# Preparing the first feed-forward tile one row group per block instead of in seven neighbouring segments

## The chip, the cores and the metric

The kernel runs on one core of a Trainium2 chip. The metric is the device time of one execution in microseconds. The core has five instruction streams that the profile shows: PE (matrix products), DVE (VectorE), ACT (ScalarE), POOL (GpSimd) and SP (SyncE, which here issues nearly all DMAs). Each stream runs its instructions in the order in which the program writes them; streams meet through semaphores.

## What is computed

A transformer layer on 2048 rows of width 640 in bf16. First comes an attention with a recurrent memory: the rows are cut into 64 segments of 32, each segment is put behind 8 memory rows, and the first 8 rows of its output are the memory of the next segment. So segment s+1 can't begin its projections of the memory rows before segment s has its output.

```python
for s in range(n_seg):                       # 64 segments of 32 rows, one after the other
    h = concat([mem, x_ln[s*32:(s+1)*32]])   # 8 + 32 rows
    q, k, v = h @ Wq, h @ Wk, h @ Wv         # 32 heads of 128
    o = softmax(mask(q @ k.T * scale)) @ v @ Wo
    mem = o[:8]; outs.append(o[8:])
h  = x + concat(outs)
h2 = h + (relu(layernorm(h) @ w1 + b1) ** 2) @ w2 + b2     # 640 -> 1728 -> 640
```

Both layer norms are over the 640 columns of a row, without gain or bias.

## The kernel before, in words

**Segments and blocks.** Four segments make a block of 128 rows (16 blocks, loop over `b` at L911, over `sp` 0 to 3 below it; the segment number is `i = 4*b + sp`). A call of `step(b, sp)` writes the instructions of one segment. Its main chain goes: projections q and k on PE, evacuated by ACT into `row` and turned by DVE into `qT` and `kT`; POOL spreads `qT` into `qz`; PE makes the scores of the memory rows (`sm`); DVE and ACT make the softmax; PE multiplies by the values (`po`) and by the output weights (`pw`); and DVE and ACT turn the new memory into the operand of the next segment (`otr`, `otc`, `hT`, L294 to L297). A segment's stretch of time is counted here from its predecessor's first `otr` to its own.

**Queues of small work.** Work that is not in that chain stands in Python lists of closures, run at fixed places of `step`: `fill` holds PE work (the rows of each segment whose keys and values do not depend on the memory are projected a block ahead in the first, second and third segments; the fourth has the output product of the block before), `late` is emptied near the start of a step (L469: two items at the start, ten in blocks 0, 14 and 15; L552: one more after the first two projections; L560: the rest before the last), and `mid` gives two items at the end of a step (L678), after the instructions that hand the memory to the next segment. So what stands in `mid` in segment i runs at the start of the stretch of segment i+1, between `rk` (L653) and `o` (L285). `soon` gives one closure before each step (L913). The layer norm of block b+1's input has its statistics in `late` of the first segment of block b, its normalisation (`ln_norm`, L188, into `xn`) in `late` of the second and its DMA transpose (L193) before the third. In the second segment `tails_v_in` (L417) issues four loads into `vt`, in the third `load_x` one.

**The first feed-forward tile.** The feed-forward part works on tiles of 512 rows (`NT`), each of four groups of 128 (`NK4`). The rows of the first tile have been known since block 3, and while the attention still runs they are prepared. One group k takes five steps, and the loop at L956 says in which segments they are put: `prep_load` (SP: two DMAs, the attention's rows from `o_all`, L764, and the input rows, L765); one segment later `prep_sum` at the step's end (DVE, 128x640, L771); two segments later the statistics near the start (`stats`: DVE two `BATCH_NORM_STATS2` L170 and one aggregate L172, then POOL two operations on 128x1, L174 and L175) and the normalisation at the end (DVE, L776, into `hn`); three segments later, before the step, the DMA transpose into `hnT0` (SP, L193). `hn` takes the same single buffer as `xn` (tag `xn` in a pool of one), so a normalisation of either kind waits until the transpose of the one before has read it. From the end of segment 60 on, `early_units` computes three columns of the first feed-forward product from `hnT0` as `fill`.

Of the kernel before, what the change touches and what calls it, by code (L numbers as in the profile page):

```python
# [16 lines left out]
def kernel(  # L17
# [28 lines left out]
    NS = S // SEG  # L46
# [89 lines left out]
    def load_x(b, eng=nc.sync):  # L136
        xt = s2.tile([128, D], BF16, tag="xt", name="xt")
        r0 = b * 128 - (M if b else 0)
        eng.dma_start(out=xt[:], in_=x2d[r0:r0 + 128, :])
        xts[b] = xt  # L140
# [40 lines left out]
    def ln_stats(b):  # L181
        xns[b] = stats(xts[b][:])

    def ln_norm(b):
        mv, rs = xns[b]
        xn = s1.tile([128, D], BF16, tag="xn", name="xn")
        xt = xts.pop(b)
        nc.vector.tensor_scalar(out=xn[:], in0=xt[:], scalar1=mv[:, 0:1], scalar2=rs[:, 0:1],  # L188
                                op0=ALU.subtract, op1=ALU.mult)
        xns[b] = xn  # L190
# [4 lines left out]
    def ln_turn(b):  # L195

        xn = xns.pop(b)
        if isinstance(b, tuple):
            hTt = ht0[2][:].rearrange("p (c b k s) -> p c b k s", c=DC, b=4, k=TL)
            dma_transpose(hTt.rearrange("p c b k s -> p c (b k s)"), xn[:])  # L200
            hTts[b[1]] = hTt
            return
        if b not in hT4s:
            hT4s[b] = s2.tile([128, DC, 4, SEG], BF16, tag="hT4", name="hT4")
        dma_transpose(hT4s[b][:].rearrange("p c s t -> p c (s t)"), xn[:])
# [95 lines left out]
    def run(q, n):  # L301
        while n > 0 and q:
            q.pop(0)()
            n -= 1
# [4 lines left out]
    def tail_units(b, which, tiles=(mmtile, mmtile)):  # L309
        w = {"q": wq, "k": wk, "v": wv}[which]  # L310
        lhs = lambda c: tail_rows(b, c)
        st = {}

        def unit(n, c):
            def f():
                if c == 0:
                    st[n] = tiles[n]()
                proj(w, "columns" if which != "v" else "order", lhs, n, st[n], c, c + 1)
                if c == DC - 1:
                    tail_out(b, which, n, st[n][:])  # L320
            return f
        return [unit(n, c) for n in range(2) for c in range(DC)]

    def tail_quarters(b, which, n, u):
        if which == "v":
            wr = wv[:].rearrange("p (c k n u f) -> p c n k u f", c=DC, k=G, n=2, u=2)
            cols = lambda c, k: wr[:, c, n, k, u]
        else:
            w = {"q": wq, "k": wk}[which]
            wr = w[:].rearrange("p (c g j n k e) -> p c n k g j e", c=DC, g=G, n=2, j=4, k=4)  # L330
            cols = lambda c, k: wr[:, c, n, k, 2 * u:2 * u + 2]
        st = {}

        def unit(cs):
            def f():
                if 0 in cs:
                    st["ps"] = mmtile()
                for c in cs:
                    for k in range(4):
                        matmul(st["ps"][32 * k:32 * k + 32, 0:256], lhsT=tail_rows(b, c), rhs=cols(c, k),  # L340
                               start=(c == 0), stop=(c == DC - 1))
                if DC - 1 in cs:
                    row = spare.pop(0) if spare else rowtile()
                    evac_row(which, row[:, 0:256], st["ps"][:, 0:256])
                    if which == "v":
                        nc.sync.dma_start(out=vt_d[b, 2 * n + u], in_=row[:, 0:256])
                        return
                    dst = tails[b][which]
                    late.append(lambda: nc.vector.transpose(out=dst[:, n * 16 + u * 8:n * 16 + u * 8 + 8, 0:32],
                                                            in_=row[:, 0:256].rearrange("p (h e) -> p h e", e=32)))  # L350
            return f
        return [unit(cs) for cs in ((0, 1), (2, 3), (4,))]
# [22 lines left out]
    def wo_tail_units(b, tile_=mmtile):  # L375
        st = {}

        def out():
            o = wo_out(st["ps"])
            dst = o_all[:].rearrange("(b s t) d -> b s t d", s=4, t=SEG)  # L380
            for ch in range(2):
                nc.sync.dma_start(out=dst[b, :, HD:SEG, ch * DH:(ch + 1) * DH], in_=o[32 * ch:32 * ch + 32, :])

        def unit(k):
            def f():
                if k == 0:
                    st["ps"] = tile_()
                wo_rounds(lambda p: oTts[b % 2][:, p, :], st["ps"], k * 16 // 10, (k + 1) * 16 // 10)
                if k == 9:
                    late.append(out)  # L390
            return f
        return [unit(k) for k in range(10)]
# [304 lines left out]
    def ffn_biases():  # L697
        nc.sync.dma_start(out=b1b[:, 0:FFULL], in_=B_b1[0:FFULL * 128].rearrange("(c p) -> p c", p=128))
        for hh in range(2):
            nc.sync.dma_start(out=b1b[FREM * hh:FREM * (hh + 1), FFULL:FC],  # L700
                              in_=B_b1[FFULL * 128:F].rearrange("(p o) -> p o", o=1))
# [111 lines left out]
    def prep_sum0(k):  # L813
        pre[k] = prep_sum(0, k, pre[k])

    def prep_stats0(k):
        pre[k] = (pre[k], stats(pre[k]))

    def prep_norm0(k):
        hn = prep_norm(0, k, pre[k][0], *pre[k][1])  # L820
        soon.append(lambda: prep_turn(0, k, hn))
# [89 lines left out]
    for b in range(NB):  # L911
        for sp in range(4):
            run(soon, 1)  # L913
            if sp == 2 and b + 2 < NB:
                load_x(b + 2)
            if b == 0:
                for h in range((3, 1, 1, 1)[sp]):
                    fill += halves.pop(0)
                if sp:
                    fill += tail_quarters(*quarters.pop(0))  # L920
                if sp < 3:
                    soon.append(lambda n=(8, 5, 5)[sp]: [stores.pop()() for _ in range(min(len(stores), n))])
                if sp == 1:
                    late.append(lambda: ln_stats(("t", 3)))
                    mid.append(lambda: ln_norm(("t", 3)))
                if sp == 2:
                    ln_turn(("t", 3))
                    late.append(lambda: ln_stats(1))
                    mid.append(lambda: ln_norm(1))
                if sp == 3:  # L930
                    ln_turn(1)
                    spare += [hnT0[:, c, :] for c in range(2)]
            elif b < NB - 1:
                if sp == 0:
                    fill += tail_units(b + 1, "q")[0:DC] + tail_quarters(b + 1, "q", 1, 0)
                if sp == 1:
                    parts = tail_units(b + 1, "k")
                    fill += tail_quarters(b + 1, "q", 1, 1) + parts[0:DC]
                if sp == 2:
                    fill += parts[DC:]  # L940
                    if quarters:
                        fill += tail_quarters(*quarters.pop(0))
            if sp == 3 and b > 0:
                fill += wo_tail_units(b - 1)
            if b > 0 and sp == 0 and b + 1 < NB:
                late.append(lambda b=b: ln_stats(b + 1))
            if b > 0 and sp == 1 and b + 1 < NB:
                late.append(lambda b=b: ln_norm(b + 1))
            if b > 0 and sp == 2 and b + 1 < NB:
                ln_turn(b + 1)  # L950
            i = b * 4 + sp
            if (b, sp) == (1, 0):
                ffn_biases()
            if (b, sp) == (2, 2):
                nc.gpsimd.tensor_copy(out=b1f[:], in_=b1b[:])
            for k in range(NK4):  # L956
                at = NS - 12 + k + k // 3
                if i == at:
                    pre[k] = prep_load(0, k)
                if i == at + 1:  # L960
                    mid.append(lambda k=k: prep_sum0(k))
                if i == at + 2:
                    late.append(lambda k=k: prep_stats0(k))
                    mid.append(lambda k=k: prep_norm0(k))
            if i == NS - 4:
                early_places()
            if NS - 4 <= i < NS - 1:
                fill += early_units(i - (NS - 4))
            step(b, sp, v0 if b + sp == 0 else None)
# [23 lines left out]
    for t in range(S // NT):  # L993
# [6 lines left out]
        for fc in range(0 if t else NE, FC):  # L1000
# [14 lines left out]
            if more and fc >= first and (fc - first) // 3 < NK4:  # L1015
                k, stage = divmod(fc - first, 3)
# [16 lines left out]
        for q in range(NK4):  # L1033
# [8 lines left out]
            for hh in range(2):  # L1042
                k = pr + 2 * hh
# [46 lines left out]
```

## Time and profile before

| | us |
|---|---|
| median of three executions | 954.45 (953.89, 954.45, 956.87) |
| the profiled execution | 954.3 |
| its span, first to last instruction | 952.5 |
| PE busy in the span | 928.0 |
| DVE, ACT, POOL busy | 700.6, 545.6, 258.1 |
| granted TensorE clock, mean | 0.996 |
| the four `hn` normalisations begin | 713.3 to 765.2 |

The page of the profile shows busy time for each engine, the chain of work that ended last (followed back from the last instruction to what released each step), and groups of instructions by line, with the idle time of the engine before them and what ended it. The trace behind it can be asked for busy time in any stretch of time, for the chain in order of time, and for the instructions in order of time. L-numbers are lines of the kernel. `q8` is the DMA queue that fetched instruction code most (202 packets, 3.31 MB).

### The profile page before, as it was taken

The numbers are of one execution on the slowest core, as the hardware profiler recorded it, in microseconds if no ns is written. First come the engines' busy times: TensorE is split into PE (matmuls) and PEld (weight loads), VectorE is DVE, ScalarE is ACT, GpSimd is POOL, SyncE is SP. The second block draws the span as 40 slices with busy tenths as digits, with TensorE's granted clock in tenths as the row PEclk, the third lists the DMA queues.
The fourth block names the chain that finished last, engine by engine and source line by source line (L and its number), as shares of the span: only waits on it lengthen the run. The fifth ranks groups of instructions, "written<-read, shape, count | busy, mean of one in ns | idle before, by whom it ended". The sixth has DMA issues, their size and how long they took to land.

```text
span 952.5 us, 57527 instructions
## 1 busy us (share of the span) xinstructions
PE 928.0 (97%) x25861; PEld 574.9 (60%) x25873; DVE 700.6 (74%) x2136; ACT 545.6 (57%) x1342; POOL 258.1 (27%) x798
## 2 busy tenths in 40 slices
PE   6989999999999999999999999999999999999998
PEld 2455766666666666666666566666665566555555
DVE  3267888888888888888888888888888777476532
ACT  2546666666666666666666666666665666523321
POOL 1013222222222222222222222222223322164300
PEclk9989999999999999999999999999999999999999
DMA  9973210101010101010101010101021110463220
GB/s 352 398 245 91 46 29 17 27 13 30 14 29 10 34 11 33 9 35 9 34 9 34 9 34 9 34 10 31 25 59 39 32 36 7 133 174 90 90 56 29
DMA packets 63334, 57.23 MB, mean 60 GB/s; under 512 B 29544, under 2 KB 59248, under 8 KB 61168
## 3 DMA queue, kind: packets, MB, share of 16 engines
q1 hardware_dynamic: 62400, 53.23, 18.6%
q8 instruction: 202, 3.31, 1.5%
q14 instruction: 44, 0.36, 0.1%
q10 hardware_dynamic: 688, 0.33, 0.1%
HBM read 38.86 MB, written 9.44 MB: 51 GB/s over the span
## 4 chain that ended last, share of the span: by engine, by line
PE 88%; DMA 5%; DVE 3%; ACT 1%; SPq 1%; issue 1%; DVEq 0%; ACTq 0%
PE ps L114 59%; PE pw L114 16%; PE y L114 6%; PE po L114 5%; DMA wv<-in_A_Wv_dram 1%; DMA vt_d<-row 1%; PE sm L114 1%; DMA wo<-in_A_Wo_dram 1%; DMA vt<-vt_d 1%; SPq L163 1%; DVE qT L266 1%; DVE kT L489 0%; ACT row L263 0%; DVE kT L266 0%; ACT row L261 0%
## 5 line engine op out<-in xcount | busy, mean ns | idle before, releaser
L114 PEld LDWEIGHTS <-hT 128*32 128x32 bf16 x8348 | 222.5, 96 | 128.2 <-DVE hT L297 6.1
L114 PE MATMUL pw<-wo,oT 128*32 128x320 bf16 x4224 | 181.0, 302 | 3.3 <-DMA wo<-in_A_Wo_dram 2.9
L114 PE MATMUL ps<-wv,hT 128*32 128x512 bf16 x2520 | 177.6, 380 | 0.0
L114 PE MATMUL ps<-wq,hT 128*32 128x512 bf16 (+1 forms) x3138 | 160.2, 337 | 0.3 <-DVE hT L297 0.3
L114 PE MATMUL ps<-wk,hT 128*32 128x512 bf16 (+1 forms) x2570 | 159.7, 375 | 0.1
L114 PEld LDWEIGHTS <-oT 128*32 128x32 bf16 x4224 | 97.6, 96 | 58.9 <-DVE oT L252 20.1
L655 POOL TENSOR_TENSOR pkt<-ek,rk 128x64 bf16<-128x64 bf16 x64 | 19.1, 299 | 413.2 <-DVE rk L653 413.2
L261 ACT ACTIVATE row<-ps 128x512 bf16<-128x512 f32 (+1 forms) x170 | 94.0, 562 | 12.4 <-PE ps L114 8.8
L266 DVE STREAM_TRANSPOSE qT<-row 128x512 bf16<-128x512 bf16 x128 | 89.8, 701 | 9.7 <-ACT row L261 6.2
L443 ACT CAST oT<-po 128x512 bf16<-128x512 f32 x128 | 74.8, 587 | 0.0
L1012 ACT ACTIVATE wv<-ps,b1f 128x512 bf16<-128x512 f32 (+1 forms) x53 | 35.4, 672 | 65.3 <-PE ps L114 62.8
L295 ACT COPY otc<-otr 64x40 f32<-64x40 f32 x126 | 28.0, 222 | 69.7 <-DVE otr L294 69.1
L454 POOL COPY qz<-qT 128x96 bf16<-128x96 bf16 x126 | 33.4, 265 | 118.6 <-DVE mx L505 59.6
L114 PEld LDWEIGHTS <-hTt 128*32 128x32 bf16 x1660 | 46.4, 98 | 31.3 <-issue 3.6
L114 PEld LDWEIGHTS <-v 32*128 32x128 bf16 x4064 | 42.3, 91 | 32.8 <-issue 18.6
L263 ACT CAST row<-ps 128x512 bf16<-128x512 f32 (+1 forms) x111 | 60.2, 558 | 1.6 <-PE ps L114 0.8
L629 DVE TENSOR_REDUCE zk<-ek 128x8 f32<-128x320 bf16 x64 | 31.1, 486 | 38.1 <-ACT ek L628 38.1
L114 PE MATMUL y<-wq,wk 128*128 128x320 bf16 (+1 forms) x424 | 59.0, 300 | 0.0
L486 ACT CAST row<-ps 128x256 bf16<-128x256 f32 x126 | 40.7, 375 | 30.8 <-PE ps L114 30.8
L611 ACT CAST v<-ps 128x512 bf16<-128x512 f32 x63 | 36.9, 585 | 29.7 <-PE ps L114 29.7
L114 PEld LDWEIGHTS <-qz 128*32 128x32 bf16 x2016 | 36.6, 95 | 28.4 <-POOL qz L454 4.7
L266 DVE STREAM_TRANSPOSE kT<-row 128x512 bf16<-128x512 bf16 x65 | 45.7, 702 | 10.2 <-ACT row L263 7.5
(125 smaller groups left out, 1634.0 us busy)
## 6 DMA issues: line engine op xcount, KB each, us to landing
wv<-in_A_Wv_dram SPq DMA_DIRECT2D x5, 1024.0 KB
wq<-in_A_Wq_dram SPq DMA_DIRECT2D x5, 1024.0 KB
wk<-in_A_Wk_dram SPq DMA_DIRECT2D x5, 1024.0 KB
vt<-vt_d SPq DMA_DIRECT2D x60, 64.0 KB
xt<-in_A_x_dram SPq DMA_DIRECT2D x18, 160.0 KB
wo<-in_A_Wo_dram SPq DMA_DIRECT2D x2, 1280.0 KB
wq<-in_B_w_dram SPq DMA_DIRECT2D x1, 2080.0 KB
o_all<-o SPq DMA_DIRECT2D x128, 15.0 KB
```

The lines of the kernel that those rows point to most:

```text
L114: nc.tensor.matmul(*a, **k)
L261: nc.scalar.mul(out=row, in_=ps, mul=scale)
L263: nc.scalar.copy(out=row, in_=ps)
L266: nc.vector.transpose(out=dst[:, n * 16:(n + 1) * 16, 0:32], in_=row.rearrange("p (h e) -> p h e", e=32))
L295: nc.scalar.copy(out=tc_[:, a], in_=tr[64:128, a, :, 0:M])
L443: nc.scalar.copy(out=oTg[:, n, :, :, M:NK], in_=po[:, :, n * 128:(n + 1) * 128].rearrange("p g (j q) -> p g j q", q=32))
L454: nc.gpsimd.tensor_copy(out=d.rearrange("p a (j f) -> p a j f", j=3)[:, :, :, 0:M], in_=src[:, :, 0:3, :])
L486: nc.scalar.copy(out=row[:, u * 256:(u + 1) * 256], in_=ps[:, u * 256:(u + 1) * 256])
L611: nc.scalar.copy(out=v[:, 512:1024], in_=ps1[:])
L629: nc.vector.tensor_reduce(out=zk[:], in_=ek[:], op=ALU.add, axis=AX.X)
L655: nc.gpsimd.tensor_tensor(out=pkt[:], in0=ek[:, :, SEG:NK], in1=rk[:].unsqueeze(2).to_broadcast([128, HG, TL]), op=ALU.mult)
L1012: nc.scalar.activation(out=r[:, 0:w], in_=ps[:, 0:w], func=ACT.Relu, bias=b1f[:, fc:fc + 1], scale=1.0)
```

## The change

The segment in which group k's steps begin is set by one line. Before, `at = NS - 12 + k + k // 3` with `NS = 64` gave 52, 53, 54 and 56. Now it gives 45, 49, 53 and 57, always the second segment of blocks 11, 12, 13 and 14:

```diff
             for k in range(NK4):
-                at = NS - 12 + k + k // 3
+                at = NS - 19 + 4 * k
                 if i == at:
                     pre[k] = prep_load(0, k)
                 if i == at + 1:
                     mid.append(lambda k=k: prep_sum0(k))
                 if i == at + 2:
                     late.append(lambda k=k: prep_stats0(k))
                     mid.append(lambda k=k: prep_norm0(k))
```

| step of group k = 0, 1, 2, 3 | segments before | segments after |
|---|---|---|
| two loads, before the step | 52, 53, 54, 56 | 45, 49, 53, 57 |
| sum, at the end | 53, 54, 55, 57 | 46, 50, 54, 58 |
| statistics, near the start; normalisation, at the end | 54, 55, 56, 58 | 47, 51, 55, 59 |
| transpose, before the step | 55, 56, 57, 59 | 48, 52, 56, 60 |

The functions that the steps call, with what they compute and into which buffers, stay as they are.

## The prediction

> **What bounds the kernel now.** The page first: PE is busy nearly throughout, and the chain that ended last is PE's for 88%.
>
> ```profile
> span 952.5 us, 57527 instructions
> PE 928.0 (97%) x25861; PEld 574.9 (60%) x25873; DVE 700.6 (74%) x2136; ACT 545.6 (57%) x1342; POOL 258.1 (27%) x798
> ...
> PE 88%; DMA 5%; DVE 3%; ACT 1%; SPq 1%; issue 1%; DVEq 0%; ACTq 0%
> ```
>
> So moving DVE work can pay only where PE stood still for it. The second view is busy time by stretch, one stretch for each segment from 46 to 59, cut at each first `otr`. The columns are the stretch, its length, then busy time and instructions of PE, PEld, DVE, ACT and POOL, the clock, the DMA share and GB/s.
>
> ```profile
> 603.53:615.56 12.03, 11.95 (x387) 7.08 (x379) 9.84 (x31) 7.78 (x20) 3.17 (x11) 1.00 0.19 35
> 615.56:627.62 12.06, 12.06 (x400) 9.49 (x396) 9.45 (x30) 7.79 (x20) 3.15 (x11) 1.00 0.05 13
> 627.62:639.92 12.30, 12.30 (x392) 7.12 (x387) 9.97 (x32) 7.36 (x19) 3.90 (x13) 1.00 0.04 10
> 639.92:651.73 11.81, 11.81 (x388) 7.20 (x383) 9.81 (x31) 7.81 (x20) 3.17 (x11) 1.00 0.09 29
> 651.73:663.54 11.81, 11.81 (x386) 7.06 (x378) 9.83 (x30) 7.77 (x20) 3.16 (x11) 1.00 0.16 35
> 663.54:675.48 11.94, 11.94 (x399) 7.70 (x395) 9.45 (x30) 7.78 (x20) 3.17 (x11) 1.00 0.05 12
> 675.48:687.64 12.16, 12.16 (x391) 7.23 (x386) 9.85 (x32) 7.36 (x19) 3.89 (x13) 1.00 0.13 37
> 687.64:699.65 12.01, 12.01 (x390) 9.23 (x385) 9.89 (x32) 7.81 (x20) 3.17 (x11) 1.00 0.19 56
> 699.65:712.09 12.44, 12.17 (x386) 7.03 (x378) 10.87 (x34) 7.67 (x20) 3.98 (x13) 1.00 0.23 60
> 712.09:724.14 12.05, 12.00 (x400) 7.86 (x396) 10.54 (x34) 7.77 (x20) 4.18 (x13) 1.00 0.12 26
> 724.14:737.69 13.55, 12.41 (x391) 7.51 (x386) 11.54 (x37) 7.17 (x19) 4.97 (x15) 1.00 0.18 45
> 737.69:751.97 14.28, 12.05 (x388) 7.42 (x383) 10.06 (x32) 7.81 (x20) 3.19 (x11) 1.00 0.14 36
> 751.97:763.99 12.02, 11.95 (x386) 7.25 (x378) 10.60 (x34) 7.78 (x20) 3.97 (x13) 1.00 0.12 21
> 763.99:775.88 11.89, 11.58 (x399) 7.61 (x395) 9.76 (x30) 7.50 (x19) 3.19 (x11) 1.00 0.10 21
> ```
>
> From 46 to 53 PE is never idle for more than 0.08 us a stretch. In 54 to 58 it stands 0.27 + 0.05 + 1.14 + 2.23 + 0.07 = 3.76 us. The last line, segment 59, is short although it carries a normalisation. Third, the chain in order of time in segment 57, the worst:
>
> ```profile
> 738.99 0.32 DVE hn L776
> ...
> 740.58 2.66 DMA hnT<-hn
> ...
> 743.68 0.06 DVE xn L188
> ```
>
> Group 2's transpose is issued at the start of segment 57, where the block's own `ln_norm` wants the same single buffer. DVE waits 2.7 us for it, with the `qT` and `kT` turns queued behind.
>
> **The change, part by part.**
>
> What it removes. The five stretches 54 to 58 last 12.44 + 12.05 + 13.55 + 14.28 + 12.02 = 64.34 us. Undisturbed stretches of the same kinds are, from the table, third segment 12.03 or 11.81, fourth 12.06 or 11.94, first 12.30 or 12.16, second 11.81 or 12.01. With the longer of each the five would take 60.43, with the shorter 59.53: they give back 3.9 to 4.8 us. I take the middle, 4.36, since which of the two belongs to which place follows the code's position and I can't tell it. Two causes lie in it: the transpose wait of 57 (14.28 against 11.91, 2.4 us), and in 54 to 56 too much DVE work at once. Segment 56 takes a normalisation (0.40), a sum (0.59) and two sets of statistics (1.05 each), the block's own and group 2's; it is 1.3 us long of its kind.
>
> What it adds, for each group:
>
> - Loads (SP, 0.35 to 0.59 and 0.43 us of issue) now stand in the second segment ahead of the four `vt` loads of L417 (0.6 each). These land about 0.9 us later, and `vt` is first read in the next block, three segments on: nothing. What is left is the traffic. The nearest row is segment 53, which had such a load and took 12.01 where 49 took 11.81, so between 0 and 0.2 in each of the two stretches that are new to it and outside the five (45 and 49). I take 0.1 each, half, since no row shows the load as the cause: 0.2 us (0 to 0.4).
> - Sum (0.44 us alone, L771) and statistics (0.44 + 0.46 + 0.21, less overlap 1.05 us of DVE, and 0.22 + 0.57 on POOL) now lie in the stretches of the fourth segments, which have the least DVE work of the four kinds (9.45 us of some 12). The two lines that decide are these, of the instructions in order of time, from the undisturbed segment 51 and from 55:
>
> ```profile
> 665.15 0.48 DVE L285 TENSOR_TENSOR o<-pw,otmp 64x320 bf16<-64x320 f32 x1 [0.31 <-ACT otmp L284]
> ```
> ```profile
> 713.62 0.59 DVE L771 TENSOR_TENSOR ht<-old,ht 128x640 bf16<-128x640 bf16 x1
> ...
> 715.15 0.83 DVE L170 BATCH_NORM_STATS2 lnst<-ht 128x6 f32<-128x320 bf16 x2
> ```
>
>  Before `o` DVE waits for ACT anyway, and the sum fits in that place. Statistics stand ahead of the first `qT` turn, which they delay by 0.6 to 0.8 us. Segment 55 is a fourth segment with a sum, statistics and a normalisation on top, at the very places where a group's will stand; it took 12.05 against 11.94 and 12.06. So the price is between -0.01 and 0.11 a group. The `po` product that PE waits for came 7.91 us into 55 and 7.79 into 51; without the 0.31 that the normalisation held DVE, most of that 0.12 is gone. I take 0.03, so 0.1 for four (0 to 0.44).
> - Normalisation (0.40 us) at the start of the first segments' stretches: it ends before ACT's copy lets `o` begin, as in segment 59, where `o` starts 1.61 us in with it and in 51 without it. Segment 59 took 11.89. Zero; if ACT came earlier, 0.3 each.
> - Transpose (SP 1.2 us of issue, 2.66 to its reader): it waits for `hn` on SP and holds back the stores behind it (L382), whose source is a ring of five buffers. Its buffer's next writer is `ln_norm` at the start of the next segment, about 12 us after the normalisation, so some 8 us to spare. The last one is needed by the early product, which began at 787.9; `hn` would be made near 777.1 and land by 782 on that clock. Zero; if 8 us were lost, one for one.
>
> POOL sees the same instructions; in 55 the spread into `qz` ended 5.47 us into the stretch and PE took it at 5.51. That margin is thin, and without the normalisation it grows by about 0.2.
>
> Sum: -4.36 + 0.2 + 0.1 = -4.06. The profiled execution took 954.3 (span 952.5 and 1.8 around it), so 950.24; the median of the runs shown is 0.15 higher: **950.4 us**. Changes under 0.3% (2.9 us, above 951.6) are about what a measurement of this kernel can't tell from none.
>
> **Rivals.**
>
> B, DVE is still late in the four fourth segments. Sum and statistics alone made segment 54 longer by 12.44 - 11.92 = 0.52. If the fourth segments pay that, 4 x 0.52 = 2.1, less the 0.1 counted: 952.4, same. For it speaks the thin `qz` margin; against it, 55, and 0.4 us less DVE work in the fourth segments than in the third (9.45 against 9.83).
>
> C, the moved traffic delays PE's code. Undisturbed first segments differ by up to 0.6 us with no preparation near; here the third is segment 12:
>
> ```profile
> 195.12:207.88 12.76, 12.35 (x392) 7.63 (x388) 10.11 (x33) 7.35 (x19) 3.91 (x13) 1.00 0.04 10
> ```
>
>  If each of the four transposes or loads brings about such a stretch, 4 x 0.6 = 2.4: 952.8, same. For it: PE idle with nothing shown to wait for. Against it: segment 12 had DMA busy 4% only, and 675.48 with a load at 13% took 12.16. [...]
>
> D, the other side: the DVE queue has no cover at all. Then each group pays its whole 0.44 + 1.05 + 0.40 = 1.89 us on the path, in front of `o` and the first `qT`, 7.6 for four: 954.45 - 4.36 + 7.6 = 957.7, slower by 0.34%. It decides from (4.36 + 2.9) / 4 = 1.8 us a group on. Against it: segments 55 and 59 carried these very steps for 0.1 us or less.
>
> **How the numbers follow.** A, the sum, 0.80; B 0.10; C 0.06; D 0.04. A by itself reaches from -4.8 with nothing added to -3.9 with 0.4 + 0.44 added, and 0.3 on both sides for the difference between runs: 949.3 to 951.7. The range takes in B and C: 949.3 to 952.8. A little of A lies above 951.6, so faster 0.77, same 0.19, slower 0.04.
>
> **What would show it.** In the trace after: stretches 54 to 58 at 11.8 to 12.3 each, no `xn` waiting for `hnT`, PE idle there under 0.2 a stretch; fourth segments 47, 51, 55 and 59 at 11.9 to 12.1 with some 10.4 us of DVE; 45 and 49 within 0.2 of 11.81. The prediction is wrong if `sm` waits for `qz`, or `po` for `pTm`, by more than 0.3 us in those fourth segments, or if first or second segments lengthen with PE waiting for nothing shown.

## The result, and the profile after

The changed kernel took 949.26 us, the median of six executions (947.0 to 951.39); beside them the kernel before took 954.34 (six, 953.04 to 956.87). The ratio is 0.9945 with a 95% interval of 0.9926 to 0.9963, so 5.1 us less (3.5 to 7.1). Forecast were 950.4 and a range from 949.3: faster, as said, by 1.1 us more than said, and just outside the range.

The page after:

```profile
span 945.2 us, 57539 instructions
...
PE 925.9 (98%) x25873; PEld 568.4 (60%) x25873; DVE 699.1 (74%) x2136; ACT 547.6 (58%) x1342; POOL 257.8 (27%) x798
...
PE 93%; DMA 4%; SPq 1%; ACT 1%; issue 0%; DVE 0%; DVEq 0%; ACTq 0%
```

DVE was 3% of the chain that ended last before; now it is under 0.5%. Busy time by stretch in the changed kernel (columns as before: the stretch, its length, busy time and instructions of PE, PEld, DVE, ACT, POOL, then clock, DMA share, GB/s), here segments 45, 47, 48 and 54 to 59:

```profile
589.19:601.01 11.82, 11.82 (x391) 7.21 (x386) 9.80 (x32) 7.84 (x20) 3.19 (x11) 1.00 0.21 58
...
612.82:624.76 11.94, 11.94 (x400) 7.68 (x396) 10.30 (x33) 7.80 (x20) 3.98 (x13) 1.00 0.05 13
624.76:636.93 12.17, 12.17 (x392) 7.22 (x388) 10.17 (x34) 7.38 (x19) 3.94 (x13) 1.00 0.11 23
...
696.47:708.29 11.82, 11.82 (x387) 6.97 (x378) 9.83 (x31) 7.80 (x20) 3.18 (x11) 1.00 0.15 35
708.29:720.23 11.94, 11.94 (x400) 7.68 (x396) 10.29 (x34) 7.80 (x20) 3.98 (x13) 1.00 0.05 12
720.23:732.53 12.30, 12.30 (x391) 7.10 (x386) 10.27 (x33) 7.38 (x19) 3.94 (x13) 1.00 0.11 23
732.53:744.55 12.02, 11.94 (x387) 7.24 (x383) 9.90 (x31) 7.83 (x20) 3.18 (x11) 1.00 0.18 56
744.55:756.78 12.23, 12.20 (x388) 8.05 (x380) 9.84 (x31) 7.82 (x20) 3.17 (x11) 1.00 0.10 21
756.78:768.67 11.89, 11.58 (x399) 7.61 (x395) 10.23 (x33) 7.52 (x19) 3.99 (x13) 1.00 0.02 7
```

The five stretches that were 64.34 us long are 60.31 (11.82 + 11.94 + 12.30 + 12.02 + 12.23). The stretches that took the work over (45 a load, 47 a sum and statistics, 48 a normalisation and a transpose) are not lengthened by it: PE is busy to the end of each. The chain in segment 57, where the transpose wait was, is PE's but for 0.08 us; it begins:

```profile
732.48 5.73 PE ps L114 x117
738.21 0.09 PE sm L114 x16
```

All sixteen stretches of segments 45 to 60 took 196.32 us before and 191.66 after, 4.66 less. The rest of the difference of the two profiled spans (7.3 us) lies elsewhere, 1.3 us of it ahead of the first segment; the profiled execution of the changed kernel is the shortest of its six (947.0 us), that of the kernel before (954.3) lies at the median of its kind.

### The profile page after: what moved, and what is told of

Its sections match the earlier page's. It is cut to its first block, busy times and chain, and to the rows that moved or that the text cites. A ratio compares the mean times of both kernels' runs of the same rounds, so it can differ in the third digit from the quotient of the medians.

```text
span 945.2 us, 57539 instructions
## 1 busy us (share of the span) xinstructions
PE 925.9 (98%) x25873; PEld 568.4 (60%) x25873; DVE 699.1 (74%) x2136; ACT 547.6 (58%) x1342; POOL 257.8 (27%) x798
## 4 chain that ended last, share of the span: by engine, by line
PE 93%; DMA 4%; SPq 1%; ACT 1%; issue 0%; DVE 0%; DVEq 0%; ACTq 0%
PE ps L114 64%; PE pw L114 16%; PE y L114 6%; PE po L114 5%; DMA wv<-in_A_Wv_dram 2%; DMA vt_d<-row 1%; PE sm L114 1%; DMA wo<-in_A_Wo_dram 1%; SPq L163 1%; DMA vt<-vt_d 1%; SPq L132 0%; ACT row L263 0%; ACT oTt L263 0%; PE pa L114 0%; ACT hTt L218 0%
## 5 line engine op out<-in xcount | busy, mean ns | idle before, releaser
L114 PEld LDWEIGHTS <-hT 128*32 128x32 bf16 x8348 | 217.8, 96 | 132.1 <-DVE hT L297 5.9
L254 ACT CAST oT<-po 128x128 bf16<-128x128 f32 x63 | 16.8, 267 | 59.4 <-PE po L114 59.4
```

The source lines that it names most:

```text
L114: nc.tensor.matmul(*a, **k)
```

## The experiments

Two questions were open. Is the loss before made of the two causes that the forecast named (theory A), and is the cover in the fourth segments what it was taken for? And why is the measured gain over 5 us where the stretches show 4.7? Differences below are of medians of executions on the same chip; executions of one program on one chip spread over 2 to 8 us (2.0 for the kernel with the other buffer, 7.7 for the kernel before beside it), so each interval is wide and the stretches decide. The ratio is not exactly the quotient of the two medians.

**The size, once more.** The changed kernel itself:

> The changed kernel as it stands, for the size. Theory A (all of the gain lies in the stretches that held the preparation): the stretches of segments 45 to 60 together fall by 4.4 to 4.8 us against before, everything outside differs only by chance, and the time is 4.4 to 4.8 us below before. Rival R (part of the gain comes from elsewhere, for instance a place of the code after segment 60 or one in front of 45 that now always runs better): 5.0 us or more below before, with over 0.5 us of it at one place outside these stretches, the same place as in the first trace of the change.

Measured: 949.14 against 955.31, ratio 0.9936 (0.9913 to 0.9958), 6.2 us less. But this execution's stretches, two of which are segments 45 and 48, are not those of the first:

```profile
591.66:603.99 12.33, 12.07 (x390) 9.22 (x385) 9.88 (x32) 7.81 (x20) 3.17 (x11) 1.00 0.20 56
...
628.14:641.00 12.86, 12.35 (x392) 7.14 (x388) 10.40 (x34) 7.36 (x19) 3.94 (x13) 1.00 0.10 22
```

The same program took 12.17 in segment 48 in one execution and 12.86 in the other. In the latter PE stood 0.51 us between two matmuls of the block's output product, with nothing shown to wait for. Segments 45 to 60 took 194.49 here. So a single trace's stretch is undisturbed length plus chance. Theory A fits neither on size (6.2 and not 4.4 to 4.8, which its interval of 4.0 to 8.3 still allows) nor on stretches; rival R fits on size, but its fixed place isn't there.

**The wait alone.** In the kernel before, group 2's normalised rows go to a buffer that is dead by then:

```diff
-        hn = s1.tile([128, D], BF16, tag="xn", name="hn")[:] if t == 0 else hns[k]
+        hn = hns[k] if t else old[0] if k == 2 else s1.tile([128, D], BF16, tag="xn", name="hn")[:]
```

> The kernel before with its old schedule, but group 2's normalised rows go into a buffer that is dead by then, not into the one that the block's own normalisation needs. Theory A (two causes, the transpose wait and too much DVE work): segment 57 falls from 14.28 to 11.8 to 12.1 us, 54, 55, 56 and 58 stay at 12.4, 12.05, 13.5 and 12.0, and the time is 2.2 to 2.4 us below before. Rival W (when the wait goes, DVE work left over from 56 stands in its place): 57 stays above 12.8 and the gain is 1.4 us or less. Rival T (the wait was the whole loss): 56 falls too, 4 us or more below before.

Segments 56 and 57:

```profile
723.82:737.36 13.54, 12.40 (x390) 7.50 (x386) 11.54 (x37) 7.17 (x19) 4.97 (x15) 1.00 0.18 45
737.36:749.18 11.82, 11.82 (x388) 7.22 (x384) 10.23 (x32) 7.80 (x20) 3.20 (x11) 1.00 0.18 44
```

57 loses its 2.46 us, 56 keeps its excess: the two causes are separate, and nothing stood behind the wait. Rivals W and T fall by the stretches. The time, though, is 950.42 against 955.31, ratio 0.9946 (0.9927 to 0.9966): 3.2 us less at least, more than the 2.2 to 2.4 expected. Only the wait was taken away, so in other executions the wait cost more than the 2.46 us of the first trace.

**Group 2 alone moved**, in the kernel before.

```diff
-                at = NS - 12 + k + k // 3
+                at = (52, 53, 49, 56)[k]
```

(The three old buffers are taken when the first group loads, whichever it is.)

> The kernel before with group 2 alone moved, to the segments that group 1 has in the changed kernel (loads in 49, sum at the end of 50, statistics and normalisation in 51, transpose before 52). Theory A: 56 falls from 13.55 to 12.2 to 12.4 and 57 from 14.28 to 11.8 to 12.1, 54 and 58 keep their excess, 51 stays at 11.9 to 12.1; the time is 3.3 to 3.9 us below before. Rival P (56 is long because of the block's own statistics together with group 1's normalisation, not because of group 2): 56 stays above 13 and the gain is 2.2 to 2.6 us.

Segments 54, 56 and 57:

```profile
702.44:715.26 12.82, 12.56 (x386) 7.73 (x378) 10.87 (x34) 7.69 (x20) 3.97 (x13) 1.00 0.14 32
...
727.31:739.48 12.17, 12.17 (x392) 7.22 (x388) 10.16 (x34) 7.36 (x19) 3.94 (x13) 1.00 0.20 50
739.48:751.29 11.81, 11.81 (x387) 7.19 (x383) 9.90 (x31) 7.81 (x20) 3.17 (x11) 1.00 0.10 30
```

56 and 57 are free, 54 isn't, and 951.11 against 955.31 is 4.2 us less (ratio 0.9948, 0.9932 to 0.9963), a little more than A's 3.3 to 3.9. The stretches are as A has them, and rival P falls: group 2 was the cause of both long stretches.

**Every step one segment earlier** than in the changed kernel.

```diff
-                at = NS - 19 + 4 * k
+                at = NS - 20 + 4 * k
```

> The changed kernel with every step one segment earlier: sums at the end of the second, statistics and normalisation in the third segments of blocks 11 to 14, as group 0 had them in the kernel before. Theory A (the fourth segments have cover for these steps, the third have not): 46, 50, 54 and 58 each take 0.3 to 0.6 us more than the 11.82 us that they take in the changed kernel, 1.2 to 2.4 in all; the time is 2.2 to 3.5 us below before. Rival K (one group per segment is covered in any of them; what hurt in 54 was something else): 46, 50, 54 and 58 at 11.8 to 11.9, and the time as that of the changed kernel, 4.4 to 4.8 below before.

Segments 46, 50 and 58:

```profile
601.49:614.07 12.58, 12.31 (x387) 8.61 (x379) 10.88 (x35) 7.69 (x20) 3.99 (x13) 1.00 0.15 33
650.17:662.75 12.58, 12.32 (x388) 8.75 (x379) 10.87 (x35) 7.69 (x20) 3.99 (x13) 1.00 0.14 33
...
748.01:760.03 12.02, 11.95 (x387) 7.22 (x378) 10.60 (x34) 7.78 (x20) 3.99 (x13) 1.00 0.10 21
```

951.05 against 955.31, 0.9954 (0.9937 to 0.997). With 54 at 12.62 the four are 2.5 us longer than at 11.82 each: rival K falls. The time is 4.3 us less than before, outside A's 2.2 to 3.5 and near K's figure, but 1.9 us more than the changed kernel took on this chip (949.14). But 58 costs 0.2 where the others cost 0.76 to 0.8, with the same DVE instructions. In block 14 `late` gives ten items at the step's start, elsewhere two, so in 46, 50 and 54 the statistics come behind the first turns and right in front of the second `qT` turn, for which the softmax waits. That made a new theory O: the place in DVE's order decides, not the kind of segment.

**The same, with the statistics at the step's start**, on top of the edit just shown:

```diff
-            run(late, 10 if b in (0, NB - 2, NB - 1) else 2)
+            run(late, 10 if b in (0, NB - 2, NB - 1) or s in (46, 50, 54) else 2)
```

> The run with every step one segment earlier, with the statistics of groups 0 to 2 run at the step's start (in 46, 50 and 54 late gives all its items there, as in 58), so in front of the first qT turn and not in front of the second. Theory O (the place in DVE's order decides, not the kind of segment): 46, 50 and 54 take 12.0 to 12.1 us, as 58 did, where they took 12.58, 12.58 and 12.62, so 1.4 to 1.7 us less than that run in these three. Rival K2 (third segments have less room than fourth, wherever the statistics stand): 12.4 or more each.

Segments 50 and 54:

```profile
649.90:661.93 12.03, 11.96 (x388) 7.24 (x380) 10.60 (x35) 7.80 (x20) 3.97 (x13) 1.00 0.15 35
697.85:709.87 12.02, 11.95 (x386) 7.20 (x378) 10.60 (x34) 7.81 (x20) 3.98 (x13) 1.00 0.15 35
```

Theory O holds in these two; 46 took 12.38, of which 0.25 us is a stand of PE, in front of the first `sm`, that 50 and 54 don't have. 948.81 against 952.98, 0.9957 (0.9945 to 0.9969). The fourth segment's advantage in the changed kernel is mostly that two items bring its statistics out early.

**Groups 0 to 2 one segment later** than in the changed kernel.

```diff
-                at = NS - 19 + 4 * k
+                at = (46, 50, 54, 57)[k]
```

> The changed kernel with groups 0 to 2 one segment later, group 3 unmoved: sums at the end of the fourth segments, statistics and normalisation in the first segments 48, 52 and 56, where the block's own statistics are too, and the transposes before the second segments 49, 53 and 57, where the block's own normalisation wants the same buffer. Theory A (both causes of the old loss act again, three times over): 49, 53 and 57 each wait for the transpose and take 2.0 to 2.5 us more than 11.81; 48, 52 and 56 with two sets of statistics take 0.5 to 1.0 more than 12.16; 7.5 to 10.5 us more than the changed kernel in all, so 3 to 6 us above before. Rival Q (the wait cost its time only because 56 had left DVE behind): 49, 53 and 57 under 12.5, at most 3.5 us more than the changed kernel, still below before.

Segments 52, 53 and 57:

```profile
675.18:688.19 13.01, 12.53 (x391) 7.26 (x387) 11.04 (x36) 7.26 (x19) 4.73 (x15) 1.00 0.04 9
688.19:700.52 12.33, 12.14 (x389) 7.27 (x385) 10.17 (x32) 7.72 (x20) 3.20 (x11) 1.00 0.17 42
...
737.74:752.27 14.53, 12.05 (x388) 7.40 (x384) 10.06 (x32) 7.83 (x20) 3.20 (x11) 1.00 0.22 58
```

954.98 against 952.99, 1.002 (1.0007 to 1.0033): slower than before, by less than A said. Two sets of statistics in a first segment cost 0.85, as expected. The transpose wait came back whole in 57, where it cost 2.7 us, but cost only 0.41 and 0.52 in 49 and 53. There `ln_norm` stands behind the first two turns, so that PE has its first scores. Neither A nor Q as written.

**The wait left where it is, other work put in front.** The kernel before, with two items and not ten at the start of 57:

```diff
-            run(late, 10 if b in (0, NB - 2, NB - 1) else 2)
+            run(late, 10 if b in (0, NB - 2, NB - 1) and s != 57 else 2)
```

> The kernel before with one number changed: in segment 57 two items of late are run at the step's start, as in blocks 1 to 13, not ten. The block's own normalisation, which waits for group 2's transpose, then stands behind the first qT and kT turns in DVE's order and not in front of them. Theory O (what the transpose wait costs is set by what stands behind it on DVE): 57 takes 12.1 to 12.5 us where it took 14.28, so 1.8 to 2.2 us below before, with the preparation where it was. Rival M (the wait costs its length wherever it stands, because all of DVE's work is due): 57 at 13.5 or more.

Segment 57:

```profile
735.77:748.96 13.19, 12.21 (x387) 7.26 (x383) 10.17 (x32) 7.72 (x20) 3.20 (x11) 1.00 0.20 39
```

Between the two: the wait fell from 2.73 to 1.24 us and the stretch by 1.09, not by 1.8 to 2.2. The transpose was issued 3.38 us into this stretch and 2.88 into the first trace's, since SP spent 0.86 and not 0.35 us on the store ahead of it. So order is worth about half of this wait, and the buffer all of it. 950.77 against 952.98, 0.9977 (0.9968 to 0.9986): 2.2 us less, as much as O said, though the stretch shows half of that.

**The changed kernel without statistics, normalisation and transposes** of the tile, so that the first 512 output rows aren't the layer's:

```diff
-                    late.append(lambda k=k: prep_stats0(k))
-                    mid.append(lambda k=k: prep_norm0(k))
+                    pass
```

> The changed kernel without the statistics, the normalisation and the transposes of the first feed-forward tile (loads and sums stay; the first 512 rows of the output are therefore not the layer's). It gives the price that these steps still have at their new place. Theory A (none): segments 47, 48, 51, 52, 55, 56, 59 and 60 within 0.05 us of what they take in the changed kernel, and the same time, within 0.5 us. Rival S (they still cost): 0.5 us or more below the changed kernel, with the fourth segments shorter by over 0.1 each.

Segment 47:

```profile
614.28:626.22 11.94, 11.94 (x400) 7.68 (x396) 9.77 (x30) 7.80 (x20) 3.25 (x11) 1.00 0.05 13
```

11.94, as with the preparation; 51, 55 and 59 likewise. Against A, segments 48 and 52 took 12.84 and 12.57 where the changed kernel took 12.17 and 12.16. But they are longer with the work left out, and PE stood 0.49 and 0.22 us in them with nothing shown to wait for. 947.82 against 952.99, 0.9942 (0.9929 to 0.9954), about the changed kernel's ratio. At their new place these steps are free. They do use cover: without them `qz` is ready 4.42 us into segment 47, with them 5.27, and PE takes it at 5.51 in both.

**Statistics twice** in the changed kernel.

```diff
-                    late.append(lambda k=k: prep_stats0(k))
+                    late.append(lambda k=k: (stats(pre[k]), prep_stats0(k)))
```

> The changed kernel with each group's statistics computed twice in the same place (1.05 us more on DVE and 0.79 on POOL in each fourth segment). It measures how much cover is left: in the changed kernel the spread into qz ends 5.28 us into these stretches and PE takes it at 5.51. Theory A (the cover is nearly used up, 0.23 us are left): 47, 51, 55 and 59 each take 0.5 to 0.9 us more, PE idle before sm for qz, 2.0 to 3.6 in all. Rival V (another 0.8 us or more of slack exists, and the fourth segments were never near the edge): no stretch over 0.2 us longer, under 0.8 in all.

Segment 51, and the line of the waits that names the cause (total, times, longest):

```profile
661.84:674.87 13.03, 12.17 (x399) 7.82 (x395) 11.32 (x37) 7.80 (x20) 4.77 (x15) 1.00 0.04 11
```
```profile
PE sm L114 <- POOL qz L456: 3.2, 4, 0.8
```

All four fourth segments grew by 1.1 us, 4.4 in all, more than expected. In 51 `qz` came 1.16 us later (6.44 and not 5.28 us into the stretch) and PE took it 0.95 us later, so the cover was about the expected 0.23 and nothing beyond it; the stretch lost a little more behind that. 952.37 against 952.99, 0.9987 (0.9975 to 0.9999), so nearly the whole gain was gone.

**The kernel before, once more.**

> The kernel before once more, for the size of the difference and for what varies between executions of one and the same program. Theory A (4.7 us, all in the stretches of segments 45 to 60, and the rest of the measured 5 to 6 is chance): these stretches together take 195.5 to 198 us here, the excess of 54 to 58 as in the first trace to 0.3 us, and single stretches elsewhere are 0.2 to 0.8 us long at other places than in the first trace. Rival R (before has a further loss that the change removes): the same places are long again as in the first trace, and outside 45 to 60 it takes over 757 us.

953.7 against 952.98, 1.0005 (0.9996 to 1.0014). 54 and 56 are within 0.23 us of the first trace (12.67 and 13.55), but 57 took 16.06 us, so the excess is 2.0 us above the first trace's, where A allowed 0.3. The wait, and the stretch cut where the granted clock (third column from the right) changes:

```profile
DVE xn L188 <- DMA hnT<-hn: 3.3, 1, 3.3
```
```profile
734.44:744.00 9.56, 6.85 (x174) 3.88 (x170) 6.01 (x17) 5.33 (x13) 2.63 (x9) 1.00 0.20 49
744.00:747.40 3.40, 3.40 (x88) 1.59 (x82) 2.38 (x13) 1.32 (x6) 0.58 (x3) 0.50 0.02 8
747.40:750.51 3.11, 3.11 (x144) 2.26 (x138) 1.79 (x5) 1.07 (x3) 0.00 (x0) 0.99 0.02 5
```

PE stood 2.71 us for the wait, and 1.2 us after that ran at half clock for 3.4 us. Outside 45 to 60 this execution took 753.56 us, as the changed kernel did (753.55): rival R falls. What the change removes is larger than the first trace of before showed, at the same place.

**The changed kernel beside it.**

> The changed kernel once more, beside the kernel before on the same chip. Theory A: 4.0 to 5.5 us below the medians of the kernel before here, and single long stretches at other places than in the two traces so far. Rival R: 5.5 us or more below again.

947.24 against 952.98, 0.9941 (0.993 to 0.9953), 5.7 us less. Its segments 45 to 60 took 191.66, as in the first trace; the total lies beyond A's 4.0 to 5.5 by 0.2, where R has it.

**A longer wait.** The kernel before with group 2's transpose issued twice:

```diff
-        soon.append(lambda: prep_turn(0, k, hn))
+        soon.append(lambda: [prep_turn(0, k, hn) for _ in range(1 + (k == 2))])
```

> The kernel before with group 2's transpose issued twice, the second after the first, so that the block's own normalisation in segment 57 waits longer; the result is the same. In the second trace of the kernel before, PE stood idle for 2.71 us in 57 and the granted clock was then 0.5 for 3.4 us; in the first it stood 2.15 us and the clock stayed at 1. Theory G (the idle time of 57 brings half clock in a part of the executions, and the change also saves that): with over 3.5 us idle the clock is 0.5 for 3.4 us behind it in the trace, the executions' mean clocks lie at 0.996 or below in most, with 0.995 and less in over half of them (in 19 of 83 with the old wait, in none of 75 without it), and the time is 2.5 to 4.5 us above before. Rival N (the half clock in that trace had nothing to do with the wait): the clock in 57 stays at 1, the mean clocks are spread as those of before, and the time is above before by the longer wait alone, 1.2 to 2.7 us.

```profile
DVE xn L188 <- DMA hnT<-hn: 5.7, 1, 5.7
```
```profile
736.87:747.30 10.43, 5.70 (x122) 3.06 (x115) 4.47 (x13) 5.13 (x12) 1.97 (x6) 1.00 0.22 48
747.30:750.70 3.40, 3.03 (x60) 1.55 (x64) 2.67 (x10) 0.78 (x3) 1.22 (x6) 0.50 0.16 46
```

PE stood 5.10 us, and again 3.4 us of half clock began there. 959.73 against 956.25, 1.0031 (1.0016 to 1.0047). The mean clock was 0.995 or less in 9 of 12 executions; in all executions with the old wait in 57 whose clocks are on record it was in 23 of 100, and in the kernels where that wait is gone or shortened in none of 75. Theory G holds, N falls.

## Why the prediction was right or wrong

- **What bounds the kernel.** Right in the main. The five stretches lost their excess, PE is not idle in them, and `xn` no longer waits for `hnT`. The two causes are shown apart: the buffer alone frees 57, moving group 2 frees 56 and 57. That moving DVE work can pay only where PE stood still was too narrow: the five stretches lost more than the 3.76 us of idle, since their busy PE time fell too, from 60.6 to 59.55 us in the second trace of the changed kernel.
- **What it removes, 4.36.** This step failed: the term was mis-sized, 4.8 by the traces. I took the middle between two neighbours of each kind, holding that which of them applies follows the code's position. It doesn't alone: the same segment of the same program took 12.17, 12.86 and 12.30 in three executions. The lower one is the undisturbed length, what is above it chance. With the lower ones it is 64.34 - 59.53 = 4.8, and in the trace beside the second of before the five stretches took 59.55 (11.82 + 11.94 + 12.16 + 11.81 + 11.82). Forty earlier segments in the same trace would have told: their medians are 12.17, 11.81, 11.82 and 11.94.
- **What it adds, 0.3.** Zero, so this term failed too. Segments 45 and 49, with a load each, took 11.82 and 11.81 in the first trace of the changed kernel. In its other two 45 took 12.33 and 11.99, but without the load it also took 12.06 (where only group 2's normalisation had another buffer). Leaving the preparation out changes no fourth segment. That the sum fits into the wait for ACT, and the normalisation ahead of `o`, was right.
- **The range.** With 4.8 removed and nothing added the sum is 954.45 - 4.8 = 949.65, so the two terms make 0.74 of the 1.1 us. The remaining 0.4 can't be told from chance in this comparison. The 0.3 us on both sides for the difference between runs were far too small: six executions of the changed kernel spread over 4.4 us, and the interval of the gain is 3.5 to 7.1.
- **The wait of 57, taken from one execution.** The gain was 5.1, 6.2 and 5.7 in three comparisons. Each interval still takes in 4.8, but the run with the other buffer, which removes the wait alone, shows that the wait costs more than in the first trace. Two things are seen in other traces. First, the second of the two stores ahead of the transpose took 0.35 us on SP in the first trace and 0.65 to 1.03 in the five others that have them in 57, so the first trace has the shortest wait of its kind: the transpose went out 0.3 to 0.7 us later in the others. Second, in two of them the clock dropped to 0.5 for 3.4 us, 1.2 us behind the stand of 2.71 us and 0.4 us ahead of the end of that of 5.10. The sum had a term for neither. Worked out from the mean clocks, with the whole loss at 0.5 as the traces have it, an execution of before runs at half clock for 6.9 us (90 executions) and one of the changed kernel for 4.6 (17), 2.3 less. On four chips executions of before at 0.995 took 2.2, 2.2, 2.8 and 3.5 us more than those at 0.998, so 0.4 to 0.6 us for each at half clock, and the 2.3 are worth about 1 us. With the 4.66 of the stretches that makes 5.6 to 6.0, near what was measured. The 1 us is an estimate. The longer wait may be in it, since the two come together; clocks are given to 0.001, which is 1.9 us of half clock; and the clock also drops for 3.4 or 6.8 us about the first segment (6.8 in the first trace of before, 3.4 in that of the changed kernel), in most traces of either kernel. How much each of the two is worth stays open.
- **What brings the drop** stays open. In each of the 14 traces all changes of the clock lie on one grid of 3.413 us, which begins elsewhere in each trace (the clock was 0.5 from 57.63 us on for 6.826 in the first trace of before, from 59.43 on for 3.413 in that of the changed kernel). With stands of 2.71 and 5.10 us in 57 the clock dropped, with 2.15 and 2.40 it didn't. Laid on the grid of its trace, the most PE idle in one step was 2.21 and 3.41 us in the first two, 1.81 and 1.82 in the others, where the stand falls across two steps. So how a stand falls on the grid may decide; a bound on the length of the stand between 2.40 and 2.71 would fit these four cases as well. Neither is shown: about the first segment the clock dropped behind steps with 1.67 us of PE idle (before) and 1.81 (changed), no more than the 1.81 and 1.82 that brought no drop in 57.
- **Rival B** is out: the fourth segments pay nothing. My reason was partly wrong. It is mostly the place of the statistics, ahead of the first turn, that makes the fourth segments fit, and less their smaller DVE load; put there, third segments pay 0.2 and not 0.8. **C**: stretches with PE idle and nothing to wait for do occur, 0.2 to 0.7 us each, but in both kernels and at changing places; no trace ties them to the moved transfers. That they have to do with PE's code fits one finding and is not shown: the stands over 0.15 us all lie at one place of PE's instruction count modulo 256 (last section). **D** is out by the run without the preparation.

## What to carry to other kernels

Take the undisturbed length of a stage from all its repetitions, not from two neighbours, and look at a second execution before a sum is set against one trace: here a wait that idled PE for 2.2 to 2.7 us cost its length in one execution and its length and 3.4 us of half clock in another. The DVE instruction that waited for the transpose cost 2.46 us with the turns behind it in the queue, 1.09 less with the first of them in front, and nothing with a buffer of its own. So free such a buffer, or at least put the work that PE needs first in front of the wait. Statistics of 1.05 us cost nothing or 0.2 us ahead of the first `qT` turn (11.94 us in segment 47 with them and without, 12.03 in 50 for 11.82) and 0.8 ahead of the second (12.58 in 50).

## What the runs showed of the hardware that was not expected

- The granted clock fell to 0.5 for 3.4 us in segment 57 of a program that keeps PE busy for 97% of the span, after PE had stood 2.71 us (second trace of the kernel before). The drop began 1.2 us after the stand had ended, at an edge of the 3.413 us grid.
- The same program, executed again, has stretches 0.2 to 0.7 us longer at other places, with PE idle up to 0.51 us between two matmuls that wait for nothing shown. Of the stands over 0.15 us without a shown cause between segments 4 and 60 there are 30 in the 14 traces, and all 30 lie at the same place of PE's instruction count, 193 or 194 modulo 256 (in the first trace of before 0.42, 0.36 and 0.22 us, ending at 196.70, 293.00 and 532.49; in that of the changed kernel 0.20 and 0.22, ending at 338.18 and 386.79). Each trace has some 170 such places there and at most five stands. The queue `q8`, which the page lists as `instruction`, brings 202 packets of 16384 bytes for some 51800 instructions of PE, so some 256 a packet, and its packets keep step with that count: the packets begun, less a 256th of the instructions begun, stay between -1.6 and -0.6 over the whole span of both first traces. That a stand belongs to such a packet is an inference from these counts. Why such a place costs something in one execution and nothing in the next stays open.
- The second of two equal store issues on SP took 0.35 us in one execution and 0.92 in another (segment 57 of the kernel before), and the transpose behind it was issued that much later. In four other traces with these stores there it took 0.65 to 1.03.
